# Filler matmuls of a fused attention and feed-forward kernel, dealt out anew over fourteen steps

## The chip, the core and the metric

The kernel runs on one core of a Trainium2 chip. The core has a matrix engine (TensorE, PE in the profile; its weight loads are PEld), VectorE (DVE), ScalarE (ACT), GpSimd (POOL) and SyncE (SP), which issues DMAs. Each engine works through its own list of instructions in order; semaphores make one wait for another. The metric is the time of one execution in microseconds (us).

## What is computed

A layer norm, then linear attention and a SwiGLU block on the same normed input, and their sum with the input. 2048 tokens, width 512, 32 heads of 16, hidden width 1792, all in bf16:

```python
xn = _layernorm(x, axis=-1)
return x + _A_ref(xn, A_wqkv, A_wo) + _B_ref(xn, B_w_gate, B_w_up, B_w_down)

def _A_ref(x, wqkv, wo):                      # linear attention
    ...
    pq, pk = phi(q), phi(k)                   # phi: t + 1 or exp(t), plus 1e-6
    kv = jnp.einsum("bhsd,bhse->bhde", pk, v)
    z = jnp.einsum("bhsd->bhd", pk)
    num = jnp.einsum("bhqd,bhde->bhqe", pq, kv)
    den = jnp.einsum("bhqd,bhd->bhq", pq, z)[..., None] + 1e-6
    return (num / den)...reshape(B, S, D) @ wo

def _B_ref(x, w_gate, w_up, w_down):
    return (_silu(x @ w_gate) * (x @ w_up)) @ w_down
```

## The kernel before, in words

Everything stays in SBUF. The program is written as one list of operations (`K.add(engine, functions, reads, writes)`); from it every engine gets its instructions in the order of the list, with waits wherever a read or a write depends on another engine. So the order of the Python statements is the order of each engine's queue.

It runs in four stages. First (to about 48 us) the layer norm, the transposes and the projections to queries and keys. Then (48 to 68 us) a stage over 14 blocks of 128 hidden columns makes gate, up and their product for the first 384 tokens, conventionally. The other 1664 tokens go through gate and up in the third stage, the **fourteen steps** (68 to 153 us), and through the down projection in the fourth, the **pairs** (153 us to the end), both with a Strassen-Winograd scheme: seven products of sums in place of eight.

**One step** is one turn of `for fc in range(NFC)`, block `fc` of hidden columns (step 0 to 13 in this text). Tokens and contraction are cut in halves, and the work is done twice, for `q` = 0 and 1 (first and second half), each with three PSUM banks a, b, d (`GB[q]`). Products are numbered as in `prod(q, fc, bank, i, start)` (L881); each is two matmuls of 128x416. TensorE's order in a step, with who works on the results:

- product 1 into a, for both q; `seed` (ScalarE, L891) copies a to b
- product 5 into d, for both q; `keep5` (ScalarE, L896) copies d to SBUF
- for each q: product 2 onto a, then `gate0` (ScalarE, L906); product 6 onto b, then `u4` (VectorE, L916), which writes d from b and the kept copy
- **first filler place**: `fill(FILLS[fc][0])`
- for each q: product 3 onto d, which needs `u4`, then `gate1` (ScalarE, L911); product 7 onto b, then `up22` (VectorE, L921), which reads b; `h22` (POOL, L925)
- **second filler place**: `fill(FILLS[fc][1])`
- for each q: product 4 onto b, which needs `up22` to have read b; `h21` (VectorE, L931) makes the hidden block from b

That makes 28 product matmuls in a step. Product 2 needs `seed` to have read a, and the next step's `seed` overwrites b, so it needs `h21` of this step.

Other work hangs on the steps: `w_sums` (VectorE, L842), the weight sums of the next blocks; `scale` (ScalarE, L834), the scaling of later weights; `square_d` (ScalarE, L782), squares of the down weights, one each in step 2, at the end of step 3 and in step 4; `gather_d`, `total_d`, `scales_d` (end of step 6 and step 7); and the division of the attention, one tile of tokens a step in steps 0 to 10: `den_sum` (VectorE, L663) at the end of the step before, `den_turn` (VectorE, L669) after `u4`, `pq_mul` and `pz_mul` (POOL, L676 and L657), and a transpose DMA on SP's queue. From step 11 on the pairs are prepared: `bcopy` (ScalarE and POOL), `t1_part` and `t_sum` (VectorE, L1015 and L1024), `hcopy` (ScalarE, L1061), `h_sum` (VectorE, L1073). One `t1_part` stands between `u4` and `up22` in step 12 and another in step 13.

**The units that fill.** The first four tiles of 128 tokens are not in the pairs. Their outputs are made conventionally: 18 matmuls of 128x512 each, 14 of the down projection (L704) and 4 of the attention (L708), accumulated in bank 0 (tiles 0 and 2) or bank 1 (tiles 1 and 3). These 72 matmuls are the units. They wait in the list `todo` and `fill(n)` takes the next n of them, always in this order: 14 + 14 of the down projection for tiles 0 and 1, 4 + 4 of the attention for them; then 4 + 4 of the attention and 14 + 14 of the down projection for tiles 2 and 3. Unit 32 ends tile 0 and unit 36 tile 1: behind each, `oout` (VectorE, L720) adds the input and a store DMA goes to SP's queue. Units 59 to 72 read block 0 to 13 of the hidden values of tile 3, which comes from `h21` of the same step. `total_d` uses bank 0 or 1, whichever is free.

`fill(3)` in step 0 takes three more, and what is left after step 13 goes into the **passage into the pairs**:

```python
first(0)            # product 1 of pair 0 (L1089), then dseed (ScalarE, L1101)
fill(len(todo))
hcopy(1, 0)
```

After it pair 0 has attention matmuls onto bank a (L1095), which need `dseed`, products 5 and 2, attention onto d (after `dkeep`, ScalarE, L1105), product 6, product 1 of the next pair, and product 7. Between them VectorE runs a string of sums for the pair (`h_sum`, `t_sum`), then `dkeep_y` (L1109) and `du4` (L1115), which reads b; product 7 accumulates onto b after that.

Of the kernel before, what the change touches and what calls it, by code (L numbers as in the profile page):

```python
# [120 lines left out]
def bass_parallel_sum__linear_attn_block__swiglu_ffn__prompt_kernel(nc, A_x, A_wqkv, A_wo, B_x, B_w_gate, B_w_up, B_w_down, out):  # L121
# [5 lines left out]
    with contextlib.ExitStack() as es:  # L127
# [796 lines left out]
        def h22(q, fc):  # L924
            K.add("pool", lambda e: e.tensor_tensor(  # L925
                out=hj(fc)[:, TB + q * TS:TB + (q + 1) * TS], in0=c22[:, q, :], in1=sil4[:, 2 + q, :], op=ALU.mult),
                r=[("c22", q), ("sil4", 2 + q)], w=[("hj", fc, 2 + q)], a=hjold(fc))
# [10 lines left out]
        def fill(n):  # L938
            for _ in range(min(n, len(todo))):
                fn, r, w, after = todo.pop(0)  # L940
                K.add("pe", fn, r=r, w=w)
                busy[w[0]] = after is None
                if after is not None:
                    after()
# [23 lines left out]
        def prepare(text):  # L968
            for w in text.split():
                steps2[w[0]](*[int(v) for v in w[1:]])  # L970
# [159 lines left out]

        SC = {1: [("wg", 2, "act")], 2: [("wu", 3, "act")], 3: [("wg", 3, "act")], 4: [("wu", 4, "act")], 5: [("wg", 4, "act")], 6: [("wu", 5, "act")], 7: [("wg", 5, "act")], 8: [("wg", 6, "act")], 9: [("wu", 6, "act")]}
        LATE = {10: [(11, 0)], 11: [(11, 1)]}
        FILLS = ((3, 4), (2, 3), (1, 3), (3, 5), (1, 4), (1, 2), (0, 2), (2, 2), (1, 3), (1, 3), (1, 3), (1, 2), (3, 3), (6, 1))
        DIV = {i + 0: ORDER[i] for i in range(11)}
        for fc in range(NFC):
            for q in (0, 1):
# [25 lines left out]
            prepare(BESIDE.get(14 + 2 * fc, ""))  # L1162
            fill(FILLS[fc][0])
            for q in (0, 1):
# [4 lines left out]
                h22(q, fc)  # L1169
            fill(FILLS[fc][1])  # L1170
            for q in (0, 1):
# [174 lines left out]
```

## Time and profile before

| | us |
|---|---|
| runs before (three): median, lowest, highest | 200.21, 200.05, 200.54 |
| the profiled execution: its own time | 200.1 |
| its span, first to last instruction | 198.9 |
| granted TensorE clock in it | 1.000 |
| TensorE busy, in matmuls | 194.7 |
| VectorE, ScalarE, POOL busy | 172.1, 157.2, 124.0 |

Step boundaries are read off TensorE's timeline as the first matmul of product 1. In us from the span's start, steps 1 to 13 begin at 75.49, 81.49, 87.28, 93.93, 99.93, 105.58, 111.17, 117.06, 122.85, 128.63, 134.42, 140.07 and 146.29; the pairs' first matmul is at 153.01.

How to read the views. A window row gives the stretch, its length, the busy time of PE, PEld, DVE, ACT and POOL with the number of instructions, the granted clock and the DMA's share. A timeline row gives start, length, engine, line, operation, what is written and read, how many instructions are merged, and in square brackets how long the engine was idle before and what ended that. The shown length of a matmul (0.34 for 416 columns, 0.38 for 512) is longer than its distance to the next one, since matmuls are pipelined: distances are taken from start to start. Some matmul records are missing (16 weight loads of L708 against 14 matmuls), each in a place where the next start is one unit late.

### The profile page before, as it was taken

The page shows a single profiled execution, that of the slowest core. Times are in us where ns is not written, and L with a number is a line of the kernel's source. Part 1 is how long each engine was busy: PE and PEld are TensorE (multiplying, and loading weights), DVE is VectorE, ACT ScalarE, POOL GpSimd, SP SyncE. Part 2 cuts the span into 40 slices and gives each one's busy share as a digit, 9 for nine tenths or more (in the row PEclk, how much of TensorE's full clock was granted, in tenths as well). Part 3 has the DMA queues.
Part 4 walks back from the last instruction along what each step waited for, and adds up shares of the span by engine and source line. Part 5 has one row for each costly group of instructions (what it writes and reads, how often), then busy time and mean ns, then how long its engine had stood idle before and what let it go on. Part 6 is the DMA issues. An engine that isn't in the chain of part 4 may idle for free.

```text
span 198.9 us, 3554 instructions
## 1 busy us (share of the span) xinstructions
PE 194.7 (98%) x1193; PEld 114.5 (58%) x1207; DVE 172.1 (87%) x328; ACT 157.2 (79%) x314; POOL 124.0 (62%) x152
## 2 busy tenths in 40 slices
PE   8999999999999999999999999999999999999995
PEld 2344444444655545555554455555555788888884
DVE  3999999996997898886899998887987999998886
ACT  4799887699798997998988888998897968575300
POOL 3787877799999388667577667868678004413220
PEclk9999999999999999999999999999999999999999
DMA  6943457899900000111110211111000012132123
GB/s 173 357 130 81 58 107 218 229 289 373 313 4 0 3 0 0 28 30 26 28 40 13 56 26 26 26 26 31 2 0 2 3 40 66 30 79 66 44 67 120
DMA packets 28899, 15.97 MB, mean 80 GB/s; under 512 B 17232, under 2 KB 28880, under 8 KB 28880
## 3 DMA queue, kind: packets, MB, share of 16 engines
q1 hardware_dynamic: 28320, 15.28, 28.8%
q10 hardware_dynamic: 560, 0.46, 0.7%
q8 instruction: 9, 0.15, 0.3%
q14 instruction: 10, 0.08, 0.2%
HBM read 9.70 MB, written 2.10 MB: 59 GB/s over the span
## 4 chain that ended last, share of the span: by engine, by line
PE 94%; DVE 2%; DMA 1%; issue 1%; ACT 0%; POOL 0%; SPq 0%
PE pb L881 35%; PE pb L1089 16%; PE pb L443 13%; PE pb L564 9%; PE pb L492 7%; PE pb L704 5%; PE pb L1095 5%; PE pb L708 2%; DMA x_sb<-in_A_x_dram 1%; PE pb L624 0%; PE pb L696 0%; DVE pq L482 0%; PE pb L406 0%; POOL ef L471 0%; DVE stats L306 0%
## 5 line engine op out<-in xcount | busy, mean ns | idle before, releaser
L676 POOL TENSOR_TENSOR pq<-pq,rden 128x512 bf16<-128x512 bf16 x16 | 16.9, 1056 | 37.2 <-DVE rden L669 26.7
L881 PE MATMUL pb<-xnT,wgu 128*128 128x416 bf16 x112 | 26.6, 339 | 0.0
L443 PE MATMUL pb<-wqkv,xnT 128*128 128x512 bf16 x110 | 25.1, 380 | 0.2
L657 POOL TENSOR_TENSOR pz<-pq,zbc 128x512 f32<-128x512 bf16 x16 | 18.9, 1179 | 5.0 <-ACT pz L650 3.5
L911 ACT ACTIVATE zacc<-pb,iw 128x416 bf16<-128x416 f32 x28 | 16.6, 613 | 4.4 <-PE pb L881 3.5
L564 PE MATMUL pb<-xnT,wgu 128*128 128x384 bf16 x112 | 19.9, 326 | 0.1
L921 DVE TENSOR_TENSOR c<-pb,p 128x416 f32<-128x416 f32 x28 | 16.4, 589 | 3.9 <-PE pb L881 1.9
L925 POOL TENSOR_TENSOR hT<-c,zacc 128x416 bf16<-128x416 f32 x16 | 15.3, 976 | 6.7 <-DVE c L921 4.1
L471 POOL TENSOR_SCALAR ef<-ef 128x512 bf16<-128x512 bf16 x25 | 15.5, 620 | 5.8 <-ACT ef L464 5.6
L443 PEld LDWEIGHTS pb<-wqkv,xnT 128*128 128x128 bf16 x112 | 10.9, 98 | 13.4 <-DVE pk L482 0.4
L916 DVE TENSOR_TENSOR pb<-p,pb 128x416 f32<-128x416 f32 x28 | 16.3, 593 | 2.1 <-PE pb L881 0.8
L464 ACT ACTIVATE ef<-pb 128x512 bf16<-128x512 f32 x25 | 14.8, 593 | 3.9 <-PE pb L443 3.9
L509 POOL TENSOR_TENSOR zacc<-zacc,pk 128x512 f32<-128x512 f32 x13 | 16.0, 1232 | 1.0
L891 ACT ACTIVATE pb<-pb 128x416 f32<-128x416 f32 x28 | 13.4, 500 | 3.4 <-PE pb L881 2.4
L881 PEld LDWEIGHTS pb<-xnT,wgu 128*128 128x128 bf16 x112 | 10.9, 98 | 8.8 <-ACT pb L891 0.3
L906 ACT ACTIVATE zacc<-pb,iw 128x416 bf16<-128x416 f32 x28 | 15.7, 625 | 0.0
L564 PEld LDWEIGHTS pb<-xnT,wgu 128*128 128x128 bf16 x112 | 10.9, 98 | 7.0
L1089 PE MATMUL pb<-wgu,xnT 128*128 128x256 f16 (+1 forms) x112 | 14.9, 273 | 0.0
L881 PE MATMUL pb<-xnT,wqkv 128*128 128x416 bf16 x56 | 14.4, 340 | 0.2
L881 PE MATMUL pb<-GT,wqkv 128*128 128x416 f16 x56 | 14.4, 339 | 0.0
L881 PE MATMUL pb<-wo,wqkv 128*128 128x416 f16 x56 | 14.4, 339 | 0.0
L1095 PE MATMUL pb<-M,pk 128*128 128x256 bf16 x96 | 13.6, 273 | 0.0
(201 smaller groups left out, 489.3 us busy)
## 6 DMA issues: line engine op xcount, KB each, us to landing
x_sb<-in_A_x_dram SPq DMA_DIRECT2D x14, 128.0 KB, 4.1
wgu<-in_B_w_gate_dram SPq DMA_DIRECT2D x2, 896.0 KB, 5.5
wgu<-in_B_w_up_dram SPq DMA_DIRECT2D x2, 896.0 KB, 7.8
wd<-in_B_w_down_dram SPq DMA_DIRECT2D x2, 896.0 KB, 12.4
out_dram<-out_sb SPq DMA_DIRECT2D x24, 64.0 KB, 1.6
wqkv<-in_A_wqkv_dram SPq DMA_DIRECT2D x3, 256.0 KB, 4.7
wqkv<-in_A_wqkv_dram SPq DMA_DIRECT2D x1, 512.0 KB, 6.6
wo<-in_A_wo_dram SPq DMA_DIRECT2D x1, 512.0 KB, 8.3
```

The lines of the kernel that those rows point to most:

```text
L443: K.add("pe", [(lambda e, c=c: e.matmul(banks[b][:, :], src[:, c, t * P:(t + 1) * P], wqkv[:, c, col:col + D], start=(c == 0), stop=(c == ...
L509: K.add("pool", lambda e: e.tensor_tensor(out=dst, in0=acc, in1=more, op=ALU.add), r=[key, mkey], w=[dkey])
L564: fns.append(lambda e, c=c, b=b, w_=w_: e.matmul(banks[b][:, 0:T0], w_[:, c, fc * P:(fc + 1) * P], xnT[:, c, 0:T0], start=(c == 0), stop=( ...
L657: K.add("pool", lambda e: e.tensor_tensor(out=pzh[i][:, :, 0:DH], in0=heads(pq[:, t, :]), in1=heads(zbc[:, :]), op=ALU.mult), r=[("pq", t) ...
L676: K.add("pool", lambda e: e.tensor_tensor(out=heads(pq[:, t, :]), in0=heads(pq[:, t, :]), in1=rden[:, i, :][:, :, None].broadcast_to([P, N ...
L881: K.add("pe", [(lambda e, c=c: e.matmul(banks[bank][:, 0:TS], L[i][:, c, :], R[i][:, c, ts], start=(start and c == 0), stop=(c == 1), skip ...
L906: K.add("act", lambda e: e.activation(sil4[:, q, :], bk(a), ACT.Silu, scale=iw[:, 0:1]), r=[B(a), ("iw",)], w=[("sil4", q)], a=[("zacc", 0 ...
L911: K.add("act", lambda e: e.activation(sil4[:, 2 + q, :], bk(d), ACT.Silu, scale=iw[:, 0:1]), r=[B(d), ("iw",)], w=[("sil4", 2 + q)], a=[(" ...
L916: K.add("dve", lambda e: e.tensor_tensor(out=bk(d), in0=p5[:, q, :], in1=bk(b), op=ALU.subtract), r=[B(b), ("p5", q)], w=[B(d)])
L921: K.add("dve", lambda e: e.tensor_tensor(out=c22[:, q, :], in0=bk(b), in1=p5[:, q, :], op=ALU.subtract), r=[B(b), ("p5", q)], w=[("c22", q)])
L1089: K.add("pe", [(lambda e, k=k: e.matmul(split(banks[b][:, 0:HD]), L[:, k, :], cut[:, :, k * P:(k + 1) * P], start=(start and k == 0), stop ...
L1095: K.add("pe", [(lambda e, g=g: e.matmul(dk(b), pk[:, SLOT[t], g * P:(g + 1) * P], M[:, g, lo:lo + HD], start=False, stop=(g == NG - 1), sk ...
```

## The change

One table of numbers: how many units `fill` takes at the first and the second place of each of the fourteen steps.

```diff
-        FILLS = ((3, 4), (2, 3), (1, 3), (3, 5), (1, 4), (1, 2), (0, 2), (2, 2), (1, 3), (1, 3), (1, 3), (1, 2), (3, 3), (6, 1))
+        FILLS = ((3, 4), (2, 3), (1, 3), (3, 3), (1, 3), (1, 3), (1, 3), (1, 3), (1, 3), (1, 3), (1, 3), (1, 2), (2, 3), (4, 2))
```

By step, with the units taken up to its end (the three of `fill(3)` included):

| step | before | after | taken before | taken after |
|---|---|---|---|---|
| 0 to 2 | (3, 4) (2, 3) (1, 3) | the same | 19 | 19 |
| 3 | (3, 5) | (3, 3) | 27 | 25 |
| 4 | (1, 4) | (1, 3) | 32 | 29 |
| 5 | (1, 2) | (1, 3) | 35 | 33 |
| 6 | (0, 2) | (1, 3) | 37 | 37 |
| 7 | (2, 2) | (1, 3) | 41 | 41 |
| 8 to 11 | (1, 3) (1, 3) (1, 3) (1, 2) | the same | 56 | 56 |
| 12 | (3, 3) | (2, 3) | 62 | 61 |
| 13 | (6, 1) | (4, 2) | 69 | 67 |
| passage | 3 | 5 | 72 | 72 |

The units and their order are the same; only their places among the products differ. With unit 32, the adder `oout` of tile 0 and its store move from the end of step 4 into the second place of step 5. `oout` of tile 1 stays in step 6, behind the second of three units instead of the first of two. `total_d` finds the same bank free.

## The prediction

> **What bounds the kernel now.** I read the page's busy shares and its chain of waits first, then windows cut at the first matmul of each step, then TensorE's and its weight loads' timeline around each step, and last the timelines of ScalarE and VectorE there.
>
> Page, busy shares and the chain that ended last:
>
> ```profile
> PE 194.7 (98%) x1193; PEld 114.5 (58%) x1207; DVE 172.1 (87%) x328; ACT 157.2 (79%) x314; POOL 124.0 (62%) x152
> ...
> PE 94%; DVE 2%; DMA 1%; issue 1%; ACT 0%; POOL 0%; SPq 0%
> ```
>
> TensorE is the path. The change adds and removes no instruction, so its matmul time stays; it can only alter the moments in which TensorE stands still, and which of them are there must be seen below the page.
>
> Windows from step to step (columns: stretch, length, busy time of each engine); in order steps 3 to 8, 12, 13, and the passage:
>
> ```profile
> 87.28:93.93 6.65, 6.65 (x38) 3.52 (x36) 5.01 (x10) 6.08 (x12) 4.83 (x6) 1.00 0.11 22
> 93.93:99.93 6.00, 5.95 (x33) 3.17 (x33) 5.41 (x11) 6.00 (x13) 3.54 (x5) 1.00 0.11 23
> 99.93:105.58 5.65, 5.65 (x33) 2.86 (x31) 5.18 (x11) 5.09 (x10) 4.06 (x5) 1.00 0.18 46
> 105.58:111.17 5.59, 5.54 (x30) 2.69 (x30) 5.30 (x11) 4.98 (x10) 4.09 (x5) 1.00 0.12 23
> 111.17:117.06 5.89, 5.89 (x34) 3.02 (x33) 5.46 (x15) 5.08 (x10) 4.09 (x5) 1.00 0.19 47
> 117.06:122.85 5.79, 5.74 (x33) 3.07 (x33) 5.03 (x11) 5.31 (x12) 4.23 (x5) 1.00 0.11 23
> ...
> 140.07:146.29 6.22, 6.17 (x35) 3.32 (x35) 5.43 (x11) 5.39 (x11) 4.72 (x6) 1.00 0.00 1
> 146.29:153.02 6.73, 6.61 (x37) 3.32 (x36) 6.03 (x10) 5.40 (x10) 5.10 (x6) 1.00 0.00 0
> 153.02:158.58 5.56, 5.50 (x47) 4.20 (x46) 5.01 (x11) 5.29 (x8) 0.86 (x1) 1.00 0.02 4
> ```
>
> Step 8 has 4 units, step 4 has 5, step 3 has 8: 5.785, 6.003 and 6.649 us, so **a unit costs 0.216 and a step without units 4.92** (28 products of 0.176). The rest of a step's length is stall: step 5 with 3 units 0.08, step 6 with 2 units 0.24, step 7 with 4 units 0.10, step 13 with 7 units 0.30; steps 3, 4, 8 and 12 none. (Some gaps of 0.39 between two products are no stalls: a product and exactly one unit whose record is missing.)
>
> Weight loads, in the order of steps 5, 6, 13 and the passage, with what they waited for:
>
> ```profile
> 105.21 0.11 PEld L881 LDWEIGHTS pb<-wqkv,wgu 128*128 128x128 bf16 x2 [0.31 <-DVE c L921]
> ...
> 108.54 0.11 PEld L881 LDWEIGHTS pb<-xnT,wqkv 128*128 128x128 f16 x2 [0.40 <-DVE pb L916]
> ...
> 152.65 0.11 PEld L881 LDWEIGHTS pb<-wqkv,wgu 128*128 128x128 bf16 x2 [0.53 <-DVE c L921]
> ...
> 158.57 0.22 PEld L1089 LDWEIGHTS pb<-xs,zacc 128*128 128x128 f16 x3 [0.29 <-DVE pb L1115]
> ```
>
> The reader sees that each stall waits for VectorE: `up22` (L921) ahead of product 4, `u4` (L916) ahead of product 3, `du4` (L1115) in the passage. The matmul starts slip by less than the idle time of the loads: from start to start 0.069, 0.154, 0.285 and 0.173 more than the matmul takes, and 0.013 more on the next one.
>
> **The timetable of a step that is not behind.** With S its first matmul, from step 5 (S 99.93) and step 6 (S 105.58): product 2 at S+1.40; `u4` of the first half starts at S+2.31 (107.89), takes 0.60, and releases product 3 0.06 later, at S+2.97. Without a first unit TensorE is there at S+2.81 (stall 0.15, as seen), with one at S+3.03. `up22` of the second half ends at 105.16 and releases product 4 at S+5.28; with one unit ahead and two behind TensorE is there at S+5.21 (stall 0.07, as seen), with three at S+5.43. **So (1, 3) just covers, and what is above it buys nothing** unless a queue is behind.
>
> **Part 1, steps 5 to 7 become (1, 3).** Step 5 loses its 0.08, step 6 its 0.24, step 7 0.075; 0.03 around the one-column `total_d` in step 7 stays. Gain 0.395.
>
> What can come in its place is VectorE being late, since unit 32, whose adder `oout(0)` (L720, 0.69) follows it on VectorE, moves from step 4 into step 5, while `oout(1)` stays in step 6. Behind such an adder stand `h21` x2 (1.09), `w_sums` (0.68 or 0.87), `den_sum` (0.71), then the next `u4`. From the rows of the adder in step 6, laid at its new place: in step 6 `u4` starts at S+2.41 and TensorE waits 0.04; in step 7, with `gather_d` (0.16 and 0.16) in the queue too, at S+2.47, and it waits 0.05 (only one unit is ahead there, where there were two). Bounds: 0, and per step the stall seen where nothing covers, 0.15. I take 0.09 for both. An adder's store goes with it on SP's queue, ahead of that step's transpose DMA, which waits for POOL's `pq_mul` anyway (store issued at 100.15, taking 0.36, the transpose at 102.88): nothing for that.
>
> **Part 2, steps 3 and 4 lose 2 units and 1.** ScalarE's timeline at the end of step 3 and through step 4:
>
> ```profile
> 92.50 1.14 ACT L834 ACTIVATE wgu<-wgu,sw 128x1024 bf16<-128x1024 bf16 x1
> 93.54 0.94 ACT L782 ACTIVATE xs<-wd 128x896 bf16<-128x896 bf16 x1
> 94.38 0.19 ACT L782 ACTIVATION_READ_ACCUMULATOR xs<-wd 128x1 f32 x1
> 94.48 0.98 ACT L891 ACTIVATE pb<-pb 128x416 f32<-128x416 f32 x2
> ...
> 99.06 1.19 ACT L834 ACTIVATE wgu<-wgu,sw 128x1024 bf16<-128x1024 bf16 x1
> 100.71 1.00 ACT L891 ACTIVATE pb<-pb 128x416 f32<-128x416 f32 x2 [0.46 <-DVE hT L931]
> ```
>
> From 91.41 to 100.25 ScalarE has no idle time: two squares of `wd` and the scaling stand in its queue ahead of the seeds. That string hangs on product 3 of step 3, ahead of the removed units, so it does not move. TensorE starts step 4 at 93.50 instead of 93.93 and wants product 2 at 94.90; the first seed ends at 94.98 and releases at 95.04: **a new stall of 0.14**. Next late are the keeps (95.37 on) and with them `u4` at 95.95 to 96.55; product 3 at 96.66 is in time. Step 5 then starts at 99.42, its first seed at 100.25 (ScalarE busy until then), released at 100.81 against product 2 at 100.82: nothing, by a hair. Bounds: 0, if the seed is quicker; 0.43 + 0.22 if the whole cover removed was needed. I take 0.14, the row being direct.
>
> **Part 3, steps 12 and 13, and the passage.** VectorE's rows:
>
> ```profile
> 150.11 0.60 DVE L1015 SCALAR_TENSOR_TENSOR mixb<-wd,sd,wgu 128x384 f16<-128x384 bf16 x1
> 151.30 1.29 DVE L921 TENSOR_TENSOR c<-pb,p 128x416 f32<-128x416 f32 x2 [0.59 <-PE pb L881]
> 152.57 1.24 DVE L931 TENSOR_TENSOR pq<-pb,zacc 128x416 bf16<-128x416 f32 x2
> 154.16 0.63 DVE L1073 TENSOR_TENSOR xn<-wqkv,xn 128x896 f16<-128x896 bf16 x1 [0.36 <-ACT xn L1061]
> ```
>
> In step 13 VectorE sits idle for 0.59 until TensorE has gone through six units: these overshoot, and the one behind is then too few. Step 12 with (2, 3): `u4` releases at 143.15, product 3 comes at 143.31, `t1_part` ends at 144.20 as the next `up22` may start at 144.21: no stall. Step 13 with (4, 2), now 0.22 earlier: `u4` releases at 149.53, product 3 comes at 149.74; `up22` can start at 150.64, when `t1_part` (to 150.49) is done; the second `up22` ends at 151.93, product 4 stalls 0.07 in place of 0.285. Gain 0.215.
>
> In the passage VectorE is without idle time from 154.16 to 157.98 and sets `du4`, so what counts is when that string starts: it waits for ScalarE's `hcopy` (153.20 to 154.13), this for `h21` of step 13 (152.57 to 153.16), which now follows product 4 at 152.13 to 152.72: the string starts 0.44 earlier. TensorE, with two units more, reaches the attention matmuls at 154.20 (`dseed` releases at 154.02, stall 0.033 and 0.013 gone) and product 7 at 158.15 (`du4` releases at 158.14; 0.173 and 0.013 gone). Gain 0.23; bounds 0, where TensorE gains as much as VectorE, and 0.23. The last of the five units reads `h21` of step 13 and runs at 153.98, a microsecond after it. Beyond, both queues are earlier by the same 0.43; the end shifts with them.
>
> **The sum.** -0.395 + 0.09 + 0.14 - 0.215 - 0.23 = -0.61. The profiled execution took 200.1 (span 198.9, 1.2 around it): 199.5. The median of the runs is 200.21, 0.1 above it: **199.6**.
>
> On one price the Trainium skill differs from the row. "TensorE: Matmul & The Clock Gate", section "Back-to-back issue gap", gives about 131 ns for a 512-column matmul in a sustained stream with its weight loads, and 216 only for an isolated one. By 131 two units behind product 7 would leave 0.24 of stall, three 0.11, and steps 5 to 7 would end 0.3 later than I forecast, an estimate of 199.9; the windows give 0.216 and 0.07, so this gets no chance above 1 in 100, inside A below.
>
> **Rivals.** (A) *VectorE and ScalarE give part back*: both are busy for 5.0 to 5.5 of 5.785 in (1, 3) steps, and the seeds of step 5 and the `u4` of steps 6 and 7 are late by margins of 0.01 to 0.05. If each of these three costs the 0.15 of an uncovered wait and the passage gives nothing: -0.61 + 0.15 + 0.21 + 0.23 = -0.02, 200.2; middle 199.9. Against it: each margin comes from a direct row. (B) *Nothing is lost in the new places*: -0.61 - 0.09 - 0.14 = -0.84, 199.4, or 199.2 if the stalls that stay in 11 and 13 vanish too. (C) *Slower: where units are taken out, the in-order queue of ScalarE (steps 3 and 4) or VectorE (13) sets the pace.* The steps then keep their old lengths; the three units of steps 3 and 4 and the two of 12 and 13 are paid there as stall, and once more where they are added: 5 x 0.216 = 1.08. The added ones win back no more than the 0.395 of part 1: +0.68, 200.9. It decides once a release comes later than TensorE by the whole cover removed, 0.43 in step 4. For it: ScalarE has 6.08 and 6.00 us of work in the two steps, and VectorE 6.03 in step 13. Against: the seed of step 4 is late by 0.14 only, step 5 leaves ScalarE 0.5 to catch up, and VectorE's idle 0.59 in step 13 is a wait for TensorE. (D) *No effect because the units wait for their own inputs*: against it, none of the units' weight loads shows a wait.
>
> **Numbers.** Forecast 0.64, own range 199.35 to 199.85; A 0.12; B 0.05; C and its like 0.19; D nothing. This kernel's measurement can tell about 0.3% (0.60) from no change, and the forecast lies on that edge: of its 0.64 I put 0.42 on faster (the 0.09 of part 1 is within the reading of the rows and may be nothing) and 0.22 on no change. Faster 0.42 + 0.05 = 0.47; same 0.22 + 0.12 = 0.34; slower 0.19. Range 199.2 (B) to 200.6 (A whole, and the near side of C).
>
> **What would show it.** Steps 5 and 6 at 5.79 and 5.8 us, step 7 at 5.85; step 4 at 5.92 with a weight load of product 2 waiting for ACT L891; steps 12 and 13 at 6.00 and about 6.3; no wait on DVE L1115 near 158; `oout(0)` in step 5. Wrong, if step 4 exceeds 6.1, if waits for L916 over 0.2 appear in steps 6 and 7, or if product 4 in step 13 still slips by 0.2.

## The result, and the profile after

| | before | after |
|---|---|---|
| median of 9 runs each, us | 200.21 | 199.69 |
| lowest and highest | 200.05, 201.43 | 199.54, 200.21 |
| profiled execution, its span | 200.1, 198.9 | 199.89, 198.6 |
| first matmul of step 0 to the end, in the trace | 130.58 | 129.93 |

The ratio is 0.9966, with a 95% interval of 0.995 to 0.9981: 0.2 to 0.5% faster. The two profiled executions differ by only 0.21, as the second one came to step 0 later (at 68.69 us, against 68.28). From the first matmul of step 0 on, which is where the change begins to act, the difference is 0.656. That stretch is the measure for all that follows.

The page after, busy shares and the chain that ended last:

```profile
PE 194.1 (98%) x1193; PEld 115.0 (58%) x1207; DVE 172.1 (87%) x328; ACT 157.2 (79%) x314; POOL 124.4 (63%) x152
...
PE 94%; DMA 2%; DVE 1%; issue 1%; SPq 0%; POOL 0%; ACT 0%
```

The page hardly tells the two kernels apart. The windows do (stretch, length, busy time of PE, PEld, DVE, ACT, POOL; steps 3 to 8, 12, 13 and the passage up to product 7 of pair 0):

```profile
87.70:93.92 6.22, 6.22 (x36) 3.33 (x34) 5.00 (x10) 5.65 (x11) 4.41 (x6) 1.00 0.12 24
93.92:99.84 5.92, 5.87 (x32) 2.99 (x32) 5.09 (x11) 5.92 (x14) 3.54 (x4) 1.00 0.12 24
99.84:105.63 5.79, 5.79 (x33) 3.03 (x32) 5.53 (x11) 5.51 (x10) 4.62 (x6) 1.00 0.11 23
105.63:111.42 5.79, 5.74 (x33) 3.02 (x33) 5.52 (x13) 5.07 (x10) 4.09 (x5) 1.00 0.18 45
111.42:117.26 5.84, 5.84 (x34) 3.14 (x33) 5.25 (x15) 5.07 (x10) 4.08 (x5) 1.00 0.19 48
117.26:123.05 5.79, 5.74 (x33) 3.08 (x33) 5.06 (x11) 5.24 (x12) 4.10 (x5) 1.00 0.11 23
...
140.27:146.27 6.00, 5.95 (x33) 3.22 (x33) 5.43 (x11) 5.39 (x11) 4.50 (x5) 1.00 0.01 1
146.27:152.56 6.29, 6.29 (x35) 3.24 (x34) 5.83 (x10) 5.39 (x10) 5.64 (x7) 1.00 0.00 0
152.56:158.34 5.78, 5.73 (x48) 4.59 (x47) 5.14 (x11) 5.34 (x8) 0.89 (x1) 1.00 0.02 4
```

Steps 5 and 6 have the length of step 8, a step without stall. Step 4 is 5.926, 0.14 over it. Weight loads of the kernel after, in step 4 and at the end of step 13:

```profile
95.45 0.12 PEld L881 LDWEIGHTS pb<-xnT,wgu 128*128 128x128 bf16 x2 [0.38 <-ACT pb L891]
...
152.20 0.11 PEld L881 LDWEIGHTS pb<-wqkv,wgu 128*128 128x128 bf16 x2 [0.31 <-DVE c L921]
...
158.34 0.33 PEld L1089 LDWEIGHTS pb<-xs,zacc 128*128 128x128 f16 x4
```

The first is the new wait, for ScalarE's `seed`; it delays the matmul by 0.131, and the next by 0.013. The second is the old one in step 13, which now costs 0.067 in place of 0.285. The third, ahead of product 7 in the passage, is a string of loads in which the view shows no wait; from start to start the matmul is late by 0.012, where 0.173 was lost. VectorE after, from step 13 into the passage:

```profile
150.09 0.60 DVE L1015 SCALAR_TENSOR_TENSOR mixb<-wd,sd,wgu 128x384 f16<-128x384 bf16 x1
150.85 1.29 DVE L921 TENSOR_TENSOR c<-pb,p 128x416 f32<-128x416 f32 x2 [0.15 <-PE pb L881]
152.34 1.09 DVE L931 TENSOR_TENSOR pq<-pb,zacc 128x416 bf16<-128x416 f32 x2 [0.19 <-PE pb L881]
153.93 0.62 DVE L1073 TENSOR_TENSOR xn<-wqkv,xn 128x896 f16<-128x896 bf16 x1 [0.50 <-ACT xn L1061]
```

Its idle time behind `t1_part` is 0.15 where it was 0.59: TensorE now runs four units there in place of six.

### The profile page after: what moved, and what is told of

Read it like the earlier page. It is cut to its first block, busy times and chain, and to the rows that moved or that the text cites. A ratio compares the mean times of both kernels' runs of the same rounds, so it can differ in the third digit from the quotient of the medians.

```text
span 198.6 us, 3554 instructions
## 1 busy us (share of the span) xinstructions
PE 194.1 (98%) x1193; PEld 115.0 (58%) x1207; DVE 172.1 (87%) x328; ACT 157.2 (79%) x314; POOL 124.4 (63%) x152
## 4 chain that ended last, share of the span: by engine, by line
PE 94%; DMA 2%; DVE 1%; issue 1%; SPq 0%; POOL 0%; ACT 0%
PE pb L881 35%; PE pb L1089 16%; PE pb L443 13%; PE pb L564 9%; PE pb L492 7%; PE pb L704 6%; PE pb L1095 5%; DMA x_sb<-in_A_x_dram 2%; PE pb L708 2%; PE pb L624 0%; PE pb L696 0%; SPq L226 0%; DVE stats L306 0%; DVE pq L482 0%; PE pb L406 0%
## 5 line engine op out<-in xcount | busy, mean ns | idle before, releaser
L306 DVE BATCH_NORM_STATS2 stats<-x_sb 128x6 f32<-128x512 bf16 x16 | 10.8, 678 | 3.5 <-DMA x_sb<-in_A_x_dram 3.5
```

## The experiments

The numbers are lengths in the traces, "from step 0" meaning from the first matmul of step 0 to the end of the span. All edits are told against the changed kernel where nothing else is said; ratios are against the kernel before.

**Parts alone: e1 and e2.** e1 has the new numbers in steps 3 to 7 only, e2 in steps 12 and 13 (and the passage) only.

```diff
 e1, steps 12 and 13
-        FILLS = (... (1, 2), (2, 3), (4, 2))
+        FILLS = (... (1, 2), (3, 3), (6, 1))
 e2, steps 3 to 7
-        FILLS = (... (1, 3), (3, 3), (1, 3), (1, 3), (1, 3), (1, 3), (1, 3), ...)
+        FILLS = (... (1, 3), (3, 5), (1, 4), (1, 2), (0, 2), (2, 2), (1, 3), ...)
```

> Steps 3 to 7 as in the changed kernel, steps 12 and 13 and the passage as before. My theory (stalls at two waits for VectorE, minus one for ScalarE in step 4, each by its own place): from the first matmul of step 0 to the end 0.23 shorter than before (steps 5, 6, 7 win 0.08 + 0.24 + 0.045... taken from the trace of the changed kernel: step 4 costs 0.14, steps 5 to 7 win 0.36), stall of 0.285 in step 13 and of 0.17 ahead of product 7 of pair 0 back. Rival 1 (the whole gain hangs on steps 12, 13 and the passage): no change, within 0.05. Rival 2 (the whole gain hangs on steps 5 to 7): 0.65 shorter.

> Steps 3 to 7 as before, steps 12 and 13 and the passage as in the changed kernel. My theory: from the first matmul of step 0 to the end 0.43 shorter than before (0.215 in step 13, 0.22 in the passage), stalls of steps 5 to 7 as before (0.08, 0.24, 0.10). Rival 1 (the gain hangs on steps 5 to 7): no change, within 0.05. Rival 2 (the passage only takes up what steps 5 to 7 won): 0.2 shorter, with a stall ahead of product 7 left.

| | from step 0 | against before | ratio of times |
|---|---|---|---|
| e1 | 130.362 | -0.220 | 0.9996 (0.9982 to 1.001) |
| e2 | 130.155 | -0.427 | 0.998 (0.9968 to 0.9991) |
| both, the change | 129.926 | -0.656 | 0.9966 (0.995 to 0.9981) |

The parts add up to 0.647 of 0.656, so neither hides the other. In e1 the stalls of 0.285 and 0.175 are where they were; in e2 those of steps 5 to 7 (0.069, 0.154, 0.069, 0.068). By the times alone e1 could not have been told from no change.

**Where a unit stands: e3 and e5.** Steps 8, 9 and 10, which the change leaves alone, take the same four units in other places.

```diff
 e3, steps 8 to 10
-        FILLS = (... (1, 3), (1, 3), (1, 3), (1, 2), (2, 3), (4, 2))
+        FILLS = (... (0, 4), (0, 4), (0, 4), (1, 2), (2, 3), (4, 2))
 e5, steps 8 to 10
-        FILLS = (... (1, 3), (1, 3), (1, 3), (1, 2), (2, 3), (4, 2))
+        FILLS = (... (2, 2), (2, 2), (2, 2), (1, 2), (2, 3), (4, 2))
```

> Steps 8, 9 and 10 take (0, 4) in place of (1, 3), all else as in the changed kernel. My theory (product 3 is released at S+2.97, TensorE is there at S+2.81): each of the three steps 0.154 + 0.013 longer, 5.95, and the kernel 0.50 longer than the changed one. Rival (only the number of units in a step decides, since VectorE is busy for 5.0 of 5.79): 5.79 each, no change.

> Steps 8, 9 and 10 take (2, 2) in place of (1, 3), all else as in the changed kernel. My theory (product 4 of the second half is released 0.85 after the last product 7, TensorE is there after 0.78): each of the three steps 0.07 + 0.013 longer, 5.87, and from step 0 to the end 0.25 longer than the changed kernel. Rival (a unit ahead also moves VectorE's release, or only the number counts): 5.79 each, no change.

e3: 5.949 in each of the three steps against 5.787, and 130.428 from step 0, 0.502 more. e5: 5.862 in each, and 130.160, 0.234 more. By the times alone neither could have been told from the changed kernel (ratios 0.9989, 0.9979 to 0.9999, and 0.9971, 0.9948 to 0.9993). A weight load of e3 in step 8:

```profile
120.46 0.11 PEld L881 LDWEIGHTS pb<-xnT,wqkv 128*128 128x128 f16 x2 [0.40 <-DVE pb L916]
```

It is the wait for `u4` that step 6 had before, to about a nanosecond (0.154). Number and kind of the instructions are the same, VectorE is busy about as long (in step 8 5.06 us in e3 and 5.13 in e5, 5.05 in the changed kernel), and each step loses 0.16 or 0.08 as either place is one unit short.

**The new stall of step 4: e4.** The square `d0` leaves the end of step 3.

```diff
-        BESIDE = {... 14: "d6 d3", 18: "d4", 21: "d0", 22: "d2", ...}
+        BESIDE = {... 14: "d6 d3", 16: "d0", 18: "d4", 22: "d2", ...}
```

> The square d0 of the down weights moves from the end of step 3 into step 1, all else as in the changed kernel. My theory (two squares and a scaling stand ahead of the seed of step 4 on ScalarE): the stall ahead of product 2 in step 4 (0.131 + 0.013) goes, step 4 takes 5.79, and the kernel is 0.14 shorter than the changed one, steps 1 and 2 keep 6.00 and 5.79. Rival (the stall of step 4 comes from something else than the ScalarE queue, such as the fewer units themselves or VectorE): step 4 stays at 5.92; or ScalarE is then late in step 2 instead, and the 0.14 reappears there.

Step 4: 5.786, steps 1 and 2: 6.003 and 5.786, from step 0 129.806, 0.120 shorter. The other steps are as before the edit, within 0.004; of the 0.140 that step 4 gains, 0.015 comes back behind step 13, about as much as two traces of the changed kernel differ there (0.011). Ratio 0.9971 (0.9954 to 0.9989). ScalarE there:

```profile
92.63 1.14 ACT L834 ACTIVATE wgu<-wgu,sw 128x1024 bf16<-128x1024 bf16 x1
94.17 0.98 ACT L891 ACTIVATE pb<-pb 128x416 f32<-128x416 f32 x2 [0.41 <-PE pb L881]
```

The seeds now wait for TensorE, not TensorE for them. So the price of the units taken from steps 3 and 4 was the wait for ScalarE's queue: without the square in it, step 4 has no stall.

**A miss: e6.** Three swaps without a unit moved between steps.

```diff
-        FILLS = ((3, 4), ... (2, 3), (4, 2))
+        FILLS = ((4, 3), ... (2, 3), (3, 3))
-        BESIDE = {... 21: "d0", 22: "d2", ...}
+        BESIDE = {... 22: "d2", 26: "d0", ...}
```

> Three edits to the changed kernel without moving a unit across steps: step 0 (3, 4) to (4, 3), step 13 (4, 2) to (3, 3), and the square d0 from the end of step 3 into step 6. My theory: step 0 loses 0.13 (product 3 there waits for a long sum ahead of u4, product 4 for nothing), step 4 loses 0.14, step 13 loses 0.08 and gets nothing new, since u4 is released just as three units end: 129.58 from step 0 to the end against 129.93. Rival (VectorE sets these places): step 13 stalls at product 3 by up to 0.21 instead, and step 0 at product 4 by 0.1: no gain over moving the square alone (129.81).

129.744 from step 0, only 0.18 shorter; ratio 0.996 (0.9945 to 0.9975). Step 0 (7.082) and step 4 (5.787) came as expected. Step 13 won only 0.05 of its 0.08, as product 3 there now waits for `u4` (0.018, and 0.013 on the next matmul), and the passage lost 0.08 again. VectorE of e6, and its weight load ahead of product 7:

```profile
150.58 1.29 DVE L921 TENSOR_TENSOR c<-pb,p 128x416 f32<-128x416 f32 x2
152.28 1.09 DVE L931 TENSOR_TENSOR pq<-pb,zacc 128x416 bf16<-128x416 f32 x2 [0.41 <-PE pb L881]
```

```profile
158.29 0.33 PEld L1089 LDWEIGHTS pb<-xs,zacc 128*128 128x128 f16 x4 [0.20 <-DVE pb L1115]
```

With a unit less ahead, `up22` follows `t1_part` without a gap: VectorE sets the pace there, and TensorE cannot be early. With a unit more behind, `h21` waits 0.41 for product 4, and it heads the string that ends in `du4`. I had looked at product 4 and forgotten who waits for it. Step 7 also grew by 0.06 (5.908): its `u4` began 0.06 later in the step, and TensorE waited for it. In the trace the square in step 6 makes ScalarE's `gate1` late, and with it POOL's `h22`, which then ran into VectorE's `w_sums` (0.74 in place of 0.68); no run takes this apart.

**Regular throughout: e7, and what went wrong in it: e9 to e12.** e7 takes away all that is above (1, 3) in steps 1 and 3.

```diff
+        FILLS = ((4, 3), (1, 3), (1, 3), (1, 3), (1, 3), (1, 3), (1, 3), (1, 3), (1, 3), (1, 3), (1, 3), (1, 3), (2, 3), (4, 3))
+        BESIDE = {... 22: "d2", 26: "d0", ...}
```

> All steps from 1 to 11 take (1, 3), step 0 (4, 3), step 12 (2, 3), step 13 (4, 3), the passage 6, and the square d0 moves into step 6; the two adders fall into the second places of steps 6 and 7. My theory (nothing above (1, 3) buys anything where ScalarE's squares stand one to every second step): steps 1 to 11 at 5.79 each, 0.02 to 0.05 more in step 7 or 8 behind the second adder, step 13 at 6.43, no stall in the passage: 129.45 from step 0 to the end, 0.48 shorter than the changed kernel. Rival (the extra units of steps 1 and 3 cover something that shows only when they are gone, ScalarE's 5.5 to 6.1 us of work there): steps 2 to 4 stall at product 2 by 0.1 to 0.4, and the kernel is no faster than the changed one.

Steps 1 to 6 and 8 to 11 took 5.786 to 5.798, step 13 6.435, and the passage had no stall, as expected; step 7 took 5.846, a hundredth more than forecast. But step 12 took 6.417, and of the 0.48 only 0.03 was left (129.900). (The times of e7, median 199.59, ratio 0.9959, 0.9944 to 0.9973, lie lower than those of the changed kernel in the same set, 199.89, ratio 0.9977, 0.9964 to 0.999. They include the start, and one trace cannot tell whether step 12 goes this way in every execution.) Step 12 in e7 and then in the changed kernel, VectorE and then POOL each time:

```profile
142.73 1.48 DVE L1015 SCALAR_TENSOR_TENSOR mixb<-wd,sd,wgu 128x384 f16<-128x384 bf16 x1
```

```profile
142.68 1.12 POOL L828 TENSOR_SCALAR M<-M,sm 128x1024 bf16<-128x1024 bf16 x1
```

```profile
143.79 0.61 DVE L1015 SCALAR_TENSOR_TENSOR mixb<-wd,sd,wgu 128x384 f16<-128x384 bf16 x1
```

```profile
143.86 1.52 POOL L828 TENSOR_SCALAR M<-M,sm 128x1024 bf16<-128x1024 bf16 x1
```

`t1_part`, 0.61 long in the changed kernel, takes 1.48, and `up22` behind it keeps product 4 waiting (0.261 and 0.138). In the changed kernel `t1_part` started 0.07 ahead of POOL's `m_scale`, and there it was POOL that got longer, 1.52. In both, the one that began first went at its own speed. e9 was to test that: it puts both `m_scale` at the end of step 10, and e10 does this to the changed kernel.

```diff
-            if fc in [10, 11]:
-                m_scale([10, 11].index(fc))
+            if fc == 10:
+                m_scale(0)
+                m_scale(1)
```

> e7 with one edit: both m_scale operations of POOL stand at the end of step 10 (before: steps 10 and 11), so none runs while VectorE makes the t1_part of step 12. My theory of e7 (its t1_part took 1.48 in place of 0.61 because POOL's m_scale had begun 0.05 earlier and the two cannot run together): t1_part back at 0.6, the stalls of 0.261 and 0.138 ahead of product 4 in step 12 gone, step 12 at 6.00, 129.49 from step 0 to the end, 0.44 shorter than the changed kernel. Rival (step 12 was late because steps 1 to 11 had no unit to spare): step 12 stays at 6.42 and the whole at 129.90.

> The changed kernel with the same edit as e9 and nothing else. My theory: there VectorE's t1_part of step 12 began 0.07 ahead of POOL's m_scale and was not held up, so nothing changes: 129.93 from step 0 to the end, within 0.03, step 12 at 6.00. Rival (the early m_scale is worth something by itself): 0.1 or more shorter.

Both forecasts of the time were missed. e9: `t1_part` was back at 0.60, but step 12 took 6.538 (130.007 from step 0; ratio 0.9966, 0.9945 to 0.9987). e10: step 12 took 6.672, and the stretch from step 0 was 0.68 longer than in the changed kernel (130.606; ratio 1.0009, 0.9985 to 1.0033). Step 12 of e10, POOL and then VectorE:

```profile
138.31 2.22 POOL L828 TENSOR_SCALAR M<-M,sm 128x1024 bf16<-128x1024 bf16 x2
140.49 2.09 POOL L925 TENSOR_TENSOR pq<-c,zacc 128x416 bf16<-128x416 f32 x2
```

```profile
140.96 0.78 DVE L842 TENSOR_TENSOR wqkv<-wqkv,wgu 128x512 f16<-128x512 f16 x1
141.78 1.08 DVE L842 TENSOR_TENSOR wqkv<-wgu,wqkv 128x512 f16<-128x512 bf16 x1
```

The two operations of POOL push its `h22` back by a whole `m_scale` (139.48 in the changed kernel), onto VectorE's `w_sums`: 0.78 and 1.08 in place of 0.61 and 0.42. In e9 the same two took 0.58 and 1.08, and in both `u4` behind them was late. The collision was not removed, it found another pair. So e11 keeps the order of the changed kernel from step 8 on, and e12 only lets `m_scale` of e7 begin later, by one small operation of POOL.

```diff
 e11, against e7
-        FILLS = (... (1, 3), (2, 3), (4, 3))
+        FILLS = (... (1, 2), (2, 3), (4, 3))
 e12, against e7
             if fc in [10, 11]:
+                if fc == 11:
+                    K.add("pool", lambda e: e.tensor_scalar(
+                        out=nm[:, 0:1], in0=mv[:, 0, 0:1], scalar1=-1.0, scalar2=0.0, op0=ALU.mult, op1=ALU.add))
                 m_scale([10, 11].index(fc))
```

> e7 with step 11 at (1, 2) as in the changed kernel; the unit goes to the passage (7). My theory (from step 8 on the queues then stand to each other as in the changed kernel, so VectorE's t1_part of step 12 is ahead of POOL's m_scale again): step 12 at 6.00, step 11 at 5.65 with its 0.08 of stall, 129.57 from step 0 to the end, 0.36 shorter than the changed kernel. Rival (the extra units of steps 1 and 3 are needed in step 12): step 12 at 6.2 to 6.4 and 129.9.

> e7 with one small operation more on POOL, one column (0.19 for one of that kind in the trace), ahead of the second m_scale in step 11, which thereby begins 0.19 later. My theory (t1_part took 1.48 in e7 because m_scale began 0.05 ahead of it): now t1_part begins first and takes 0.6, m_scale takes 1.5, step 12 at 6.00, 129.49 from step 0 to the end: an operation added makes the kernel 0.41 shorter than e7. Rival (POOL's load as such, or the missing units): step 12 stays at 6.42 or grows by 0.19.

e11: step 12 6.002, 129.541 from step 0. e12: step 12 6.003, 129.461. Step 12 in e12, VectorE and then POOL:

```profile
142.88 0.61 DVE L1015 SCALAR_TENSOR_TENSOR mixb<-wd,sd,wgu 128x384 f16<-128x384 bf16 x1
```

```profile
142.83 0.19 POOL L1201 TENSOR_SCALAR nm<-mv 128x1 f32<-128x1 f32 x1
142.99 1.49 POOL L828 TENSOR_SCALAR M<-M,sm 128x1024 bf16<-128x1024 bf16 x1
```

An operation added on POOL makes the kernel 0.44 shorter than e7, by letting VectorE be first by 0.11. Both versions beat the kernel before: e11 199.23 (ratio 0.9948, 0.9935 to 0.996), e12 199.28 (0.9945, 0.9932 to 0.9959), beside 200.19 in the same set. The changed kernel did not run in that set; that they are shorter than it too, by 0.385 and 0.465 from step 0, is shown by the traces.

**The changed kernel again: e8.**

> The changed kernel again, beside the others on one chip. If stalls are set by the order of the queues alone, the same stalls as in its first profile, each within 0.01 (0.131 in step 4, 0.069 in 11, 0.067 in 13), 129.93 within 0.02 from step 0 to the end, and what differs between executions lies ahead of step 0. If they depend on the chip or the execution, the stalls differ by 0.05 and more.

129.941 from step 0 (129.926 the first time), and the stalls are the same: 0.133, 0.069 and 0.071. What differs is the start: step 0 began at 69.22 in place of 68.69.

## Why the prediction was right

- **The sum.** Forecast -0.61 (199.6), measured -0.656 from step 0 in the trace and 199.69 for the median, inside the forecast's own range of 199.35 to 199.85. The 0.52 between the medians is less than the 0.60 that the prediction held to be the least that can be told, and yet the interval leaves no change out.
- **The price of a unit and the timetable of a step**, on which all else stood: 0.216 held in every step whose count of units changed, and e3 and e5 show both margins of the (1, 3) step from the other side, 0.154 and 0.069.
- **Part 1**: forecast -0.395 + 0.09. The trace has -0.36 (steps 5, 6 and 7 less the price of their units). The term that was mis-sized is the 0.09 for VectorE being late behind the adders: nothing came in step 6, and 0.035 in step 7. `u4` had been laid at S+2.41 and S+2.47 in the two steps, and began at S+2.37 and S+2.44.
- **Part 2**: 0.14 forecast, 0.139 measured, and e4 shows that it is ScalarE's queue, with the square in it. The margin of step 5 was mis-sized: its first seed was to be in time "by a hair", 0.01, and was in time by 0.19, as it began 0.15 before the end of ScalarE's scaling and not behind it.
- **Part 3**: -0.215 forecast for step 13 and -0.218 measured; -0.23 for the passage and -0.223 measured. Step 12 stayed free of stalls at (2, 3).
- **The rivals.** C fell: step 4 was late by 0.14 and ScalarE had caught up in step 5, and in step 13 VectorE still stood idle for TensorE (0.15). A fell with the passage, which gave nearly all that was forecast, and with its three margins, which cost 0, 0 and 0.035 where it put 0.15 each. B was half right, for part 1. D was never near.
- **Where it was lucky.** I laid VectorE's old row of `t_sum` (L1024, 1.38) at its new time. In the changed kernel that operation takes 0.67, and the `t1_part` behind it 1.46 where it took 0.74, because POOL now meets the second one: before, POOL's second `h22` began first (147.08, `t_sum` 147.14); after, `t_sum` did (147.13, `h22` 147.28). The two come to 2.12 and 2.13. Nothing in the working told that this would come out even. Nor did it look at POOL in step 12, where "no stall" hangs on `t1_part` beginning ahead of `m_scale`: it did by 0.09 before and by 0.07 after, and in e7, where the order turned, the step lost 0.4.

## What to carry to other kernels

Filler work is worth what it covers at the place where it stands: find for each place when the release comes and when the filled engine would be there, put just enough, and follow who waits for the instruction behind it. When a queue is shifted by tenths of a microsecond, look for pairs of operations of VectorE and GpSimd that begin within 0.1 of each other; an order that is won by 0.07 in one version is lost by 0.05 in another. Compare traces from a common mark, not by their spans, where the start varies more than the effect.

## What the runs showed of the hardware

VectorE and GpSimd held each other up in certain pairs. `t1_part`, all in SBUF, took 0.60 to 0.61 where it was not held up and 1.48 when GpSimd's `m_scale` had begun 0.05 earlier; with VectorE ahead by 0.07 to 0.11, `m_scale` took 1.49 to 1.52 in place of 1.12. `up22`, which reads one input from PSUM, ran at its usual 0.59 beside GpSimd's L1003 (150.85, after). The Trainium skill states the rule in "SBUF — State Buffer", section "SBUF: two separate sides": the two engines share a port pair as an exclusive lock that goes to whoever starts first, for operations of VectorE with two SBUF inputs among others. The runs agree on who wins.

They also show that the loser is blocked until the other has ended. A `w_sums` of 128x1024 elements, 0.68 long when nothing holds it up, ended 0.55 after `h22` did in each of three steps of the kernel after, though it had begun 0.19, 0.30 and 0.41 before that end; it took 0.74, 0.84 and 0.95. So the wait grows with the time that the other still has to go, and about 0.13 of the instruction's own length is not added to it. For `t1_part` in e7 this part is 0.2: it ended 0.40 after `m_scale`, less than its own 0.61. What an instruction does in that part, the runs do not show.

A wait of TensorE that ends late costs 0.012 to 0.014 more on the following matmul (0.131 and 0.013 in step 4, 0.067 and 0.014 in step 13).

Nearly all the difference between executions lies in the first 12 us. The first accumulation of keys (L492) began between 10.95 and 11.90 us in the fourteen traces, and from there to the first matmul of step 0 it took 57.32 in twelve of them, and 57.40 and 57.49 in two. What varies in that start was not looked into.
